# A three-stage kernel: the fold of the transform's input moves from the vector engines into the first products

## The chip, the cores and the metric

The kernel runs as one program on one core of a Trainium2 chip. The metric is the device time of one execution in microseconds (us); the figure quoted is the median of several executions.

## The reference

The reference takes `x` (8 batches, 3072 positions, 256 channels). It computes the real part of the two-dimensional discrete Fourier transform of each batch. The result, 24576 tokens of 256 numbers, goes through a dense layer pair (`softplus(x @ w_in) @ w_out`, 2048 hidden units), and then through a mixture of 8 experts: each token goes to the expert with the largest cosine similarity, and comes out as `relu(x @ w1[e]) @ w2[e]` times that expert's softmax weight.

```python
X = np.fft.fft(x, axis=1); X = np.fft.fft(X, axis=2); a = X.real
h = a @ w_in
a = (np.maximum(h, 0) + np.log1p(np.exp(-np.abs(h)))) @ w_out
e = argmax(normalised(a) @ normalised(emb).T / tau)
out = gate * (np.maximum(a @ w1[e], 0) @ w2[e])
```

## The kernel before, in words

Numbers that have to keep float32's precision are held as two float16 tiles, a high part `h` and a low part `l`, and a product of two such numbers is three TensorE products. To split a float32 tile is therefore two passes: one that scales and rounds to the high part, one that takes the difference.

**Steps.** After a start-up part, phase 1 is a loop of 256 steps, one for each unit (batch, token tile, quarter of the hidden units). Each step issues, in one order written out by hand (`ORDER`, line 56), pieces of several software-pipelined jobs: `pu` and `pv` (28 products of the dense layer's first half), `eu` (ScalarE, L806), `ev` (VectorE, L813 and L814), the softplus on ScalarE (`ab`, `ex`, `ln`: L822, L827, L831) with its last sum on VectorE (`g`, L836), the split of its result into `gh` (GpSimd, L847) and `gl` (VectorE, L860), and `G0` to `G2` (36 products of the second half). The first six steps have orders of their own (`BORD`). SBUF holds all tiles; each engine takes its instructions in this order.

**The transform** of batch b+1 runs in between, as the generator `fft_gen`, one piece at `f1` of each step and now and then one at `f2`. `fft_a` makes 16 pieces for each batch: for each of 8 input tiles `xt` (96 partitions, 4 rows of 256) it multiplies column halves c = 0 and 1 by the table `fa_s` into PSUM tile `psa`, and splits that into `U_s` (L677, L678). I call the steps with such products the A stage of a batch; the steps after them (`psb`, `psc`, `psd`, from `fft_bc`) are the B stage. The A stage of batch 0 belongs to the start-up.

**The fold.** The columns of x come in an order in which half c = 0 needs the sum of the two column halves and half c = 1 their difference. In batch 0 the products make it: per c and row six products, three with each half of the columns, the second half of c = 1 against `fan`, which is `-fa_s`. In batches 1 to 7 the tile is folded first, and per c and row there are three products. The path of one input tile through the steps is: its DMA by `x_get` (SyncE's queue, L585, two buffers `xt`); it is put on the list `late` when the products of the tile two before it are issued; in the next step `sp` folds it (`split_fold`, `x_fold`: sum and difference, L490 to L495), on VectorE for 5 or 6 of the 8 tiles (`FW`, `FW1`) and else on GpSimd with three instructions; at the end of that step `sa` scales it in place and rounds it to `xh`, two ScalarE passes (`split_hi`, L617 and L618); at the head of the step after, `sq` makes `xl` on GpSimd (`split_lo`, L610).

**GpSimd's budget.** At the top of a step `room` is set to `ROOM` (3.6) less 2.6 for a tile that waits for `sq` and 3.4 for one that waits for a fold on GpSimd. A scatter of routed rows (L960) takes 1.4 of it. The preparation of the expert weights (`wprep`, `wp` in the order) runs in chunks that take 2.1 each (L1338 with L1339, or L1343); it also stands still while `busy` is set. `unit_gh` takes 1.2 where that is left (`GPC`): it then makes the last quarter of the low part on GpSimd too (L849, L850, L851; I call it the extra split) and VectorE makes three quarters only.

**Phase 2**, the experts, follows and is not touched, apart from its first pieces, which overlap the last steps.

Of the kernel before, what the change touches and what calls it, by code (L numbers as in the profile page):

```python
# [11 lines left out]
F16 = mybir.dt.float16  # L12
# [3 lines left out]
AF = mybir.ActivationFunctionType  # L16
ALU = mybir.AluOpType
# [18 lines left out]
BOOT = "fbasabpasbpbaaaaabpfbaaaaaambstaaasaabssakaatwaobsfbskskawattaattawaaspfsatat"  # L36
FW, FA = (0, 2, 3, 6, 7), ()
OC = (0, 1, 2, 3, 4, 6, 7)
ROOM = 3.6
FW1, FA1 = (0, 2, 3, 4, 6, 7), ()  # L40
FV = (1, 4, 5, 7)
GP, GPC, GLB = (0, 1, 2, 3), 1.2, 2
# [4 lines left out]
PEF, MK, FB = True, (1, 3, 9, 11, 15), (0, 3, 6, 7)  # L47
# [95 lines left out]
def fft_moe_moe(ctx, tc, x, w_in, w128, w_out, emb, tau, w1, w2, fa, db, mcs, tid, ident, tri, misc, out,  # L143
                nbatch=NB):
    nc = tc.nc
    T, V, A, G, SY = nc.tensor, nc.vector, nc.scalar, nc.gpsimd, nc.sync
# [18 lines left out]
    p1 = ExitStack()  # L165
    pF = ExitStack()
    bigf = pF.enter_context(tc.tile_pool(name="bigf", bufs=1, side="right"))
    U_s = bigf.tile([128, 2, 2, 48, 64], F16, name="U_s")
    mcs_s = bigf.tile([128, 2, 2, 1537], F16, name="mcs_s")
    db_s = bigf.tile([128, 2, 385], F16, name="db_s")  # L170
    fa_s = bigf.tile([96, 2, 96], F16, name="fa_s")
    xp = pF.enter_context(tc.tile_pool(name="xp", bufs=2, side="right"))
    pqp = p1.enter_context(tc.tile_pool(name="pqp", bufs=9))
    big = p1.enter_context(tc.tile_pool(name="big", bufs=1))
# [22 lines left out]
    def fps(name):  # L197

        if boot[2]:
            boot[1] = (boot[1] + 1) % 4  # L200
            if boot[1]:
                return psG.tile([128, 512], F32, tag=f"G{boot[1] - 1}", name=name)
        return psF.tile([128, 512], F32, tag="F", name=name)

    def mm(o, l, r, start, stop):
        T.matmul(o, l, r, start=start, stop=stop)  # L206
# [138 lines left out]
    bootp = boot_ctx.enter_context(tc.tile_pool(name="bootp", bufs=1))  # L345
# [2 lines left out]
    ini = ini_ctx.enter_context(tc.tile_pool(name="ini", bufs=1, side="right"))  # L348
    CK = 512
    wcs = ini.tile([128, NF, 264], F32, name="wcs")  # L350
    fan = bootp.tile([96, 2, 96], F16, name="fan")
    mxw = cst.tile([128, 17], F32, name="mxw")

    def field(i, e11):
# [128 lines left out]
    scal = {}  # L483
# [3 lines left out]
    def x_fold(xt, eng):  # L487

        lo, hi = xt[:, :, 0:128], xt[:, :, 128:256]
        eng.tensor_tensor(lo, lo, hi, op=ALU.add)  # L490
        if eng is V:
            V.scalar_tensor_tensor(hi, hi, -2.0, lo, op0=ALU.mult, op1=ALU.add)
        else:
            G.tensor_scalar(hi, hi, -2.0, 1.0, op0=ALU.mult, op1=ALU.mult)
            G.tensor_tensor(hi, hi, lo, op=ALU.add)  # L495
# [82 lines left out]
    xs, ready = {}, set()  # L578

    def x_get(b, k):  # L580
        if b == 0:
            xs[b, k] = xboot[k]
            return
        xt = xp.tile([96, 4, 256], F32, tag="xt", name="xt", bufs=2)
        SY.dma_start(xt, x[b].rearrange("(p j) d -> p j d", j=32)[:, 4 * k:4 * k + 4, :])  # L585
        xs[b, k] = xt

    def x_split(b, k):
        xt = xs.pop((b, k))
        sx = scal[b]["sx"][0:96]  # L590
        xh = xp.tile([96, 4, 256], F16, tag="xh", name="xh", bufs=3)
        xl = xp.tile([96, 4, 256], F16, tag="xl", name="xl", bufs=3)
        if k not in FB:
            A.activation(xh, xt, AF.Copy, scale=sx)
            V.scalar_tensor_tensor(xl, xt, sx, xh, op0=ALU.mult, op1=ALU.subtract)
        else:
            G.tensor_scalar(xt, xt, sx, 1.0, op0=ALU.mult, op1=ALU.mult)
            G.tensor_scalar(xh, xt, 1.0, 1.0, op0=ALU.mult, op1=ALU.mult)
            G.tensor_tensor(xl, xt, xh, op=ALU.subtract)
        xs[b, k] = (xh, xl)  # L600

    def on_v(b, k):
        return k in (FW1 if b == 1 else FW)

    sp2, sp3 = [], []

    def split_lo():
        for b, k, xt, xh in sp3:
            xl = xp.tile([96, 4, 256], F16, tag="xl", name="xl", bufs=3)
            G.tensor_tensor(xl, xt, xh, op=ALU.subtract)  # L610
            xs[b, k] = (xh, xl)
        sp3.clear()

    def split_hi():
        for b, k, xt in sp2:
            xh = xp.tile([96, 4, 256], F16, tag="xh", name="xh", bufs=3)
            A.activation(xt, xt, AF.Copy, scale=scal[b]["sx"][0:96])  # L617
            A.activation(xh, xt, AF.Copy)  # L618
            sp3.append((b, k, xt, xh))
        sp2.clear()  # L620

    def split_fold():


        for b, k in late:
            xt = xs.pop((b, k))
            x_fold(xt, V if on_v(b, k) else G)
            sp2.append((b, k, xt))
        late.clear()

    def fft_pre(b):

# [11 lines left out]
    def fft_a(b):  # L644

        ph[0] = "a"
        while b not in ready:
            yield
        for k in range(8):
            if k + 2 < 8:  # L650
                x_get(b, k + 2)
            while late and late[0] == (b, k) or sp2 and sp2[0][:2] == (b, k) or sp3 and sp3[0][:2] == (b, k):
                split_lo()
                split_hi()
                split_fold()
            xh, xl = xs.pop((b, k))
            for c in range(2):
                ps = fps("psa")
                for j in range(4):
                    o = ps[:, j * 96:(j + 1) * 96]  # L660
                    cs = slice(c * 128, (c + 1) * 128)
                    if boot[0] and PEF:

                        for hf in range(2):
                            cs = slice(hf * 128, (hf + 1) * 128)
                            fs = fan if c and hf else fa_s
                            mm(o, xh[:, j, cs], fs[:, 0, :], hf == 0, False)
                            mm(o, xh[:, j, cs], fs[:, 1, :], False, False)
                            mm(o, xl[:, j, cs], fs[:, 0, :], False, hf == 1)
                        continue  # L670
                    mm(o, xh[:, j, cs], fa_s[:, 0, :], True, False)
                    mm(o, xh[:, j, cs], fa_s[:, 1, :], False, False)
                    mm(o, xl[:, j, cs], fa_s[:, 0, :], False, True)
                src = ps[:, 0:384].rearrange("p (t q) -> p q t", q=48)
                uh = U_s[:, 0, c, :, 8 * k:8 * k + 8]
                ul = U_s[:, 1, c, :, 8 * k:8 * k + 8]
                A.activation(uh, src, AF.Copy, scale=2.0 ** -16)  # L677
                V.scalar_tensor_tensor(ul, src, 2.0 ** -16, uh, op0=ALU.mult, op1=ALU.subtract)  # L678
                if c == 0 and k + 2 < 8:
# [297 lines left out]
    p2 = {}  # L977
# [379 lines left out]
    def chain(*gens):  # L1357
        for g in gens:
            yield from g

    with tc.manual_schedule():
# [5 lines left out]
        xl = x_load()  # L1367
# [23 lines left out]
        def once(fn, *a):  # L1391
            fn(*a)
            yield
# [9 lines left out]
        def need(t):  # L1403
            while step(t):
# [4 lines left out]
                  t=chain(*(once(win_split, k, h) for k in range(4) for h in range(2))), m=emb_prep(), o=wout_prep())  # L1409
# [37 lines left out]
        sc, scb = Chain(iter(())), [1]  # L1447
        fg = Chain(chain(bg["a"], fft_gen(1)) if nbatch > 1 else bg["a"])
        rq = []
        wp = Chain(iter(()))  # L1450
        for s in range(len(units) + LAG + 1):

            room[0] = ROOM - 2.6 * len(sp3) - 3.4 * sum(not on_v(*t) for t in late)
            nsc = min(len(scq), 2 if cur[0] // 8 >= npair - SNAP or len(scq) > 5 else 1) if room[0] > 0 else 0
            room[0] -= 1.4 * nsc
            busy[0] = bool(sp3) or room[0] < 2.1
            u = units[s] if s < len(units) else None
            if u is not None and u[1] == 0 and u[2] == 0 and 0 < u[0] < nbatch - 1:
                fg.gen = chain(fg.gen, fft_gen(u[0] + 1))
            if s == 4 and nbatch > 1:  # L1460
                sc = Chain(fft_first(1))
# [17 lines left out]
            if ph[0] == "b" and ph[1] + 1 < nbatch and scb[0] < ph[1] + 1:  # L1479
                end_chain(sc)  # L1480
                scb[0] = ph[1] + 1
                sc = Chain(fft_first(ph[1] + 1))
            boot[2] = s < MB
            if s == LAG + 3:
# [5 lines left out]
                wp = Chain(chain(wprep(wpp), snapshot())) if P2ON else Chain(wprep(wpp))  # L1490
# [3 lines left out]
            def x2(tt):  # L1494
                if v is not None and v[2] == 3:
                    x2_out(v[0], v[1], tt)
# [31 lines left out]
            def cv(k):  # L1528
                if s < LAG + 3:
                    wi.step(k)  # L1530
# [9 lines left out]
            def tail():  # L1540
                if "row1" in p2 and (u is None or not S2[0].get("xs")):
# [5 lines left out]
                       ln=lambda: on(unit_ln, 1), g=lambda: on(unit_g, 1), gh=lambda: on(unit_gh, 1),  # L1547
                       lv=lambda: on(unit_gl, 2),
                       G0=lambda: g2(0), G1=lambda: g2(1), G2=lambda: g2(2), x0=lambda: x2(0), x1=lambda: x2(1),
                       x2=lambda: x2(2), r1=route, r2=route, r3=route, sp=split_fold, sa=split_hi, sq=split_lo, wp=wp.step, sc=lambda: scatters(nsc), p1=tail, p2=tail, p3=tail,  # L1550
                       wo=boot_w, cb=lambda: cv(0), ck=lambda: cv(1), cp=lambda: cv(2))
            for o in BORD[s].split() if s < len(BORD) else ORDER:
                ops[o]()
# [51 lines left out]
```

## Time and profile before

| | |
|---|---|
| time, 3 executions | 3482.34 to 3485.62 us, median 3485.12 us |
| the profiled execution's own time | 3496.98 us |
| its span | 3495.2 us |
| TensorE busy | 3078.9 us, 88% of the span |
| VectorE (DVE) busy | 2796.1 us, 80% |
| ScalarE (ACT) busy | 2260.5 us, 65% |
| GpSimd (POOL) busy | 2138.7 us, 61% |
| granted TensorE clock, mean | 0.957 of full speed |

Names of engines in the rows: PE is TensorE (PEld its weight loads), DVE is VectorE, ACT is ScalarE, POOL is GpSimd, SP is SyncE. A line of a timeline gives the start, the duration, the engine, the line of the kernel, the operation, what it writes and reads, and in brackets how long the engine sat idle just before and what ended that. A line of the view of one tile gives the count and the least, the median and the longest duration in ns. All products are recorded under L206, the helper that issues them, so they are told apart by their tiles.

### The profile page before, as it was taken

Reading aid. Unit: us, or ns where it says so; the run is one execution under the profiler, and the core shown is the slowest. Engines: PE = TensorE matmul, PEld = TensorE weight load, DVE = VectorE, ACT = ScalarE, POOL = GpSimd, SP = SyncE. Lnnn points to the kernel's source line nnn. Section 1 sums busy time; section 2 is a strip of 40 time slices with the busy share of each in tenths; the row PEclk is TensorE's granted clock in tenths of the full one; section 3 lists DMA queues with packets and bytes.
Section 4 is the critical chain, followed back from the end, with each engine's and each line's share of the span. In section 5 each row is a group of like instructions: output and inputs, shape, how many; then the busy total and the mean of one; then the engine's idle time right before and its main releaser. Section 6 shows DMA issues by size and latency. Waiting matters only on the chain.

```text
span 3495.2 us, 76414 instructions
## 1 busy us (share of the span) xinstructions
PE 3078.9 (88%) x31264; PEld 2740.8 (78%) x31264; DVE 2796.1 (80%) x4488; ACT 2260.5 (65%) x3400; POOL 2138.7 (61%) x1855
## 2 busy tenths in 40 slices
PE   3788898888987988888988999998889999999997
PEld 3677787876876877777887899877778888888886
DVE  7779898988888989988988988984557777777776
ACT  5777777767877878867877888763344444444443
POOL 5357677776786777777777787662234444444443
PEclk8899998998999999999999999999899999999999
DMA  4111210311211211211111000114643333332221
GB/s 138 48 49 53 71 57 28 101 40 38 73 52 51 80 42 62 80 46 51 50 46 31 19 17 20 65 38 107 175 117 76 75 75 80 75 75 74 73 73 38
DMA packets 197088, 223.74 MB, mean 64 GB/s; under 512 B 119028, under 2 KB 154751, under 8 KB 196480
## 3 DMA queue, kind: packets, MB, share of 16 engines
q1 hardware_dynamic: 177920, 167.32, 18.1%
q0 software_dynamic: 18816, 51.54, 4.2%
q8 instruction: 244, 4.00, 0.5%
q14 instruction: 108, 0.88, 0.1%
HBM read 122.91 MB, written 70.71 MB: 55 GB/s over the span
## 4 chain that ended last, share of the span: by engine, by line
issue 29%; PE 24%; DVE 20%; POOL 12%; ACT 10%; DMA 4%; POOLq 0%; SPq 0%; DVEq 0%; ACTq 0%
PE G L206 12%; DVE e L836 5%; PE pu L206 4%; POOL out_dram L1235 3%; DVE gl L860 3%; PE pv L206 3%; ACT e L831 2%; POOL gh L847 2%; ACT e L827 2%; DVE h L814 2%; DVE h L813 2%; PE psb L206 2%; PE psH L206 1%; ACT e L822 1%; POOL xt L495 1%
## 5 line engine op out<-in xcount | busy, mean ns | idle before, releaser
L847 POOL TENSOR_SCALAR gh<-e,sc 128x1536 f16<-128x1536 f32 (+1 forms) x256 | 620.8, 2425 | 493.5 <-DVE e L836 333.2
L206 PE MATMUL G<-wo_s,gh 128*128 128x264 f16 x6144 | 832.7, 284 | 2.2 <-POOL gh L850 2.0
L206 PEld LDWEIGHTS <-gh 128*128 128x128 f16 x6144 | 602.7, 101 | 100.2 <-POOL gh L850 3.3
L206 PE MATMUL psH<-xT,wb 128*128 128x256 f16 (+1 forms) x4992 | 560.3, 274 | 67.1 <-DMA xT<-xs 66.5
L836 DVE SCALAR_TENSOR_TENSOR e<-h,e 128x1536 f32<-128x1536 f32 x256 | 531.6, 2077 | 75.3 <-ACT e L831 71.8
L206 PEld LDWEIGHTS <-wb 128*128 128x128 f16 x4992 | 480.2, 100 | 137.7 <-DMA xT<-xs 78.3
L206 PEld LDWEIGHTS <-win_s 128*128 128x128 f16 x6144 | 534.0, 100 | 24.6 <-DVE h L814 11.6
L206 PE MATMUL psO<-wb,hh 128*128 128x256 f16 x3200 | 529.8, 273 | 0.6 <-ACT hh L1209 0.6
L206 PE MATMUL G<-wo_s,gl 128*128 128x264 f16 x3072 | 440.3, 281 | 28.6 <-DVE gl L860 28.4
L1147 POOL TENSOR_TENSOR nr<-ssq,half 128x2 f32<-128x2 f32 (+1 forms) x104 | 237.5, 2284 | 355.3 <-ACT jk L1144 355.0
L860 DVE SCALAR_TENSOR_TENSOR gl<-e,sc,gh 128x1536 f16<-128x1536 f32 (+1 forms) x256 | 451.0, 1762 | 3.6 <-POOL gh L847 2.2
L206 PE MATMUL psO<-wb,hl 128*128 128x256 f16 x1600 | 436.2, 273 | 0.6 <-DVE hl L1210 0.5
L1209 ACT ACTIVATE hh<-psH 128x512 f16<-128x512 f32 (+1 forms) x416 | 239.6, 579 | 269.7 <-PE psH L206 263.8
L1210 DVE SCALAR_TENSOR_TENSOR hl<-psH,hh 128x512 f16<-128x512 f32 (+1 forms) x416 | 268.7, 666 | 181.4 <-ACT hh L1209 173.3
L822 ACT ACTIVATE e<-h 128x1536 f32<-128x1536 f32 x256 | 378.0, 1477 | 47.7 <-DVE h L814 46.7
L1235 POOL DMA_INDIRECT out_dram<-ot,r x200 | 202.3, 1011 | 311.2 <-ACT ot L1233 272.3
L831 ACT ACTIVATE e<-e 128x1536 f32<-128x1536 f32 x256 | 379.5, 1482 | 4.0
L827 ACT ACTIVATE e<-e 128x1536 f32<-128x1536 f32 x256 | 378.4, 1478 | 0.0
L206 PE MATMUL pu<-pqh,win_s 128*128 128x192 f16 (+1 forms) x2048 | 371.6, 251 | 3.8 <-ACT h L806 3.8
L206 PEld LDWEIGHTS <-gl 128*128 128x128 f16 x3072 | 303.3, 100 | 89.0 <-DVE gl L860 38.5
L206 PEld LDWEIGHTS <-hh 128*128 128x128 f16 x3200 | 312.6, 98 | 36.8 <-ACT hh L1209 0.7
L813 DVE SCALAR_TENSOR_TENSOR h<-pv,sc,h 128x768 f32<-128x768 f32 (+1 forms) x256 | 258.7, 1011 | 99.2 <-ACT h L806 50.5
(274 smaller groups left out, 5902.8 us busy)
## 6 DMA issues: line engine op xcount, KB each, us to landing
xt<-in_x_dram SPq DMA_DIRECT2D x114, 384.0 KB
r<-bucket SPq DMA_DIRECT2D x96, 268.0 KB
wt<-in_w_dram SPq DMA_DIRECT2D x16, 1024.0 KB
wsc<-wo SPq DMA_DIRECT2D x32, 512.0 KB
W<-wsc SPq DMA_DIRECT2D x32, 512.0 KB
raw<-in_w_in_dram SPq DMA_DIRECT2D x8, 512.0 KB
raw<-in_w_out_dram SPq DMA_DIRECT2D x8, 512.0 KB
wb<-wsc SPq DMA_DIRECT2D x2, 2048.0 KB
```

Source lines behind the costliest of these rows:

```text
L206: T.matmul(o, l, r, start=start, stop=stop)
L813: V.scalar_tensor_tensor(h[:, :, n:384], pv[:, :, s0:n], sc["ninv"], h[:, :, s0:n], op0=ALU.mult, op1=ALU.add)
L822: A.activation(e, h, AF.Abs)
L827: A.activation(e, e, AF.Exp, scale=-1.0)
L831: A.activation(e, e, AF.Ln, bias=1.0)
L836: V.scalar_tensor_tensor(flat(d["e"]), flat(d["h"]), 0.0, flat(d["e"]), op0=ALU.max, op1=ALU.add)
L847: G.tensor_scalar(gh[:, 0:n], e[:, 0:n], sg, 1.0, op0=ALU.mult, op1=ALU.mult)
L860: V.scalar_tensor_tensor(flat(d["gl"]), flat(d["e"]), scal[u[0]]["sg"], flat(d["gh"]), op0=ALU.mult, op1=ALU.subtract)
L1147: G.tensor_tensor(nr[:, 0:nt], ssq[:, 0:nt], half[:, 0:nt], op=ALU.pow)
L1209: A.activation(h2, p_, AF.Relu)
L1210: V.scalar_tensor_tensor(l2, p_, 0.0, h2, op0=ALU.max, op1=ALU.subtract)
L1235: no_dep(G.indirect_dma_start(out=out, out_offset=bass.IndirectOffsetOnAxis(ap=rows.bitcast(I32)[:, t, 264:265], axis=0), in_=ot, in_offse ...
```

## The change

The fold of `xt` is left out in all batches; the products make it as they do in batch 0 (six per c and row in place of three), so `fan` moves to a pool that lives through phase 1. The split becomes one ScalarE pass (`xh`, scaled and rounded, at `sa` of the step in which the tile is put on `late`) and one VectorE pass (`xl`, scaled and subtracted, at `sq` of the next step). `sp` does nothing any more. `room` starts at 4.8 in every step, and `busy` is no longer set within the loop.

```diff
-ROOM = 3.6
+ROOM = 4.8
...
+    fan = bigf.tile([96, 2, 96], F16, name="fan")
...
+    def split_hi():
+        for b, k in late:
+            xt = xs.pop((b, k))
+            xh = xp.tile([96, 4, 256], F16, tag="xh", name="xh", bufs=3)
+            A.activation(xh, xt, AF.Copy, scale=scal[b]["sx"][0:96])
+            sp3.append((b, k, xt, xh))
+        late.clear()
     def split_lo():
         for b, k, xt, xh in sp3:
             xl = xp.tile([96, 4, 256], F16, tag="xl", name="xl", bufs=3)
-            G.tensor_tensor(xl, xt, xh, op=ALU.subtract)
+            V.scalar_tensor_tensor(xl, xt, scal[b]["sx"][0:96], xh, op0=ALU.mult, op1=ALU.subtract)
             xs[b, k] = (xh, xl)
-    def split_hi():
-        for b, k, xt in sp2:
-            xh = xp.tile([96, 4, 256], F16, tag="xh", name="xh", bufs=3)
-            A.activation(xt, xt, AF.Copy, scale=scal[b]["sx"][0:96])
-            A.activation(xh, xt, AF.Copy)
-            sp3.append((b, k, xt, xh))
-    def split_fold():
-        for b, k in late:
-            xt = xs.pop((b, k))
-            x_fold(xt, V if on_v(b, k) else G)
-            sp2.append((b, k, xt))
...
-                    if boot[0] and PEF:
+                    if PEF:
                         for hf in range(2):
...
-            room[0] = ROOM - 2.6 * len(sp3) - 3.4 * sum(not on_v(*t) for t in late)
+            room[0] = ROOM
             nsc = min(len(scq), 2 if cur[0] // 8 >= npair - SNAP or len(scq) > 5 else 1) if room[0] > 0 else 0
             room[0] -= 1.4 * nsc
-            busy[0] = bool(sp3) or room[0] < 2.1
...
-  sp=split_fold, sa=split_hi, sq=split_lo
+  sp=lambda: None, sa=split_hi, sq=split_lo
```

## Rows read from the trace of the kernel before

**Rows 1.** The seven A stages, 100 steps: length, then busy time by engine

```profile
sum 895.90, PE 760.84 PEld 672.49 DVE 800.21 ACT 681.07 POOL 656.18; mean PE 108.69 PEld 96.07 DVE 114.32 ACT 97.30 POOL 93.74
```

**Rows 2.** The same, six stretches of three steps, a batch's first two tiles

```profile
sum 209.60, PE 150.87 PEld 132.66 DVE 170.44 ACT 135.72 POOL 167.56; mean PE 25.14 PEld 22.11 DVE 28.41 ACT 22.62 POOL 27.93
```

**Rows 3.** The same, the last B stage (16 steps), then 20 steps after

```profile
1983.30:2102.40 119.10, 119.10 (x1394) 110.08 (x1393) 102.27 (x118) 99.78 (x117) 95.21 (x97) 1.00 0.05 16
2108.30:2236.20 127.90, 127.90 (x1297) 117.34 (x1296) 113.37 (x112) 108.83 (x96) 96.39 (x90) 1.00 0.06 21
```

**Rows 4.** Waits from 200 to 2110 us: us in total, times, longest

```profile
ACT xt L617 <- POOL xt L495: 105.6, 17, 9.1
```

**Rows 5.** Timeline of ScalarE, one wait for a fold

```profile
534.10 1.15 ACT L617 ACTIVATE xt<-xt,sc 96x1024 f32<-96x1024 f32 x1 [6.72 <-POOL xt L495]
```

**Rows 6.** Timeline of GpSimd, the next `gh`, with VectorE out of the way

```profile
534.05 1.54 POOL L847 TENSOR_SCALAR gh<-e,sc 128x1536 f16<-128x1536 f32 x1
```

**Rows 7.** Timeline of VectorE, two sums of the softplus

```profile
589.56 3.75 DVE L836 SCALAR_TENSOR_TENSOR e<-h,e 128x1536 f32<-128x1536 f32 x1 [0.82 <-ACT e L831]
...
597.40 4.13 DVE L836 SCALAR_TENSOR_TENSOR e<-h,e 128x1536 f32<-128x1536 f32 x1
```

**Rows 8.** Timeline of GpSimd, what ran beside these two

```profile
589.53 2.15 POOL L610 TENSOR_TENSOR xl<-xt,xh 96x1024 f16<-96x1024 f32 x1
...
597.76 2.14 POOL L1343 TENSOR_TENSOR wo<-wt,wo 128x1024 f16<-128x1024 f32 x1
```

**Rows 9.** Timeline of TensorE, one set of 12 products and its follower

```profile
605.57 0.25 PE L206 MATMUL psa<-fa_s,xh 96*128 96x96 f16 x2
...
606.08 0.25 PE L206 MATMUL pu<-pqh,win_s 128*128 128x192 f16 x1
```

**Rows 10.** Tile e: instructions, count, least/median/longest ns

```profile
L836 DVE SCALAR_TENSOR_TENSOR e<-h,e x256: 1736/1759/4910, 122.2 to 2334.1; 128x1536 f32<-128x1536 f32 x128
L847 POOL TENSOR_SCALAR gh<-e,sc x256: 1217/2636/3615, 124.0 to 2338.5; 128x1152 f16<-128x1152 f32 x68, 128x1536 f16<-128x1536 f32 x60
L860 DVE SCALAR_TENSOR_TENSOR gl<-e,sc,gh x256: 1395/1804/4339, 141.4 to 2346.2; 128x1152 f16<-128x1152 f32 x68, 128x1536 f16<-128x1536 f32 x60
L849 POOL TENSOR_SCALAR e<-e,sc x115: 574/580/2301, 125.2 to 2334.0; 128x384 f32<-128x384 f32 x115
L850 POOL TENSOR_SCALAR gh<-e x115: 510/510/1886, 125.9 to 2334.7; 128x384 f16<-128x384 f32 x115
L851 POOL TENSOR_TENSOR gl<-e,gh x115: 908/916/2368, 126.5 to 2336.6; 128x384 f16<-128x384 f32 x115
```

**Rows 11.** Instructions of tile xt, and who waited for it (us, times)

```profile
L617 ACT ACTIVATE xt<-xt,sc x56: 1132/1142/1152, 212.0 to 1951.7; 96x1024 f32<-96x1024 f32 x56
...
L610 POOL TENSOR_TENSOR xl<-xt,xh x56: 2116/2142/3727, 220.9 to 1963.0; 96x1024 f16<-96x1024 f32 x56
L490 DVE TENSOR_TENSOR xt<-xt x36: 676/685/2622, 209.3 to 1948.7; 96x512 f32<-96x512 f32 x36
L492 DVE SCALAR_TENSOR_TENSOR xt<-xt x36: 686/1515/2507, 211.0 to 1949.4; 96x512 f32<-96x512 f32 x36
...
L494 POOL TENSOR_SCALAR xt<-xt x20: 613/2010/2124, 224.3 to 1924.8; 96x512 f32<-96x512 f32 x20
L495 POOL TENSOR_TENSOR xt<-xt x20: 1262/2640/2867, 225.0 to 1925.5; 96x512 f32<-96x512 f32 x20
...
  DVE xt L490: 0.2, 1
```

**Rows 12.** Instructions of tile xh: the low part on VectorE in batch 0

```profile
L595 DVE SCALAR_TENSOR_TENSOR xl<-xb,sc,xh x4: 1272/1754/3664, 31.6 to 54.4; 96x1024 f16<-96x1024 f32 x4
```

**Rows 13.** Instructions of tile pc, GpSimd's part of the B stage

```profile
L733 POOL TENSOR_SCALAR pqh<-pc x51: 505/518/2020, 182.0 to 2098.3; 128x384 f16<-128x384 f32 x44, 128x386 f16<-128x386 f32 x7
L734 POOL TENSOR_TENSOR pql<-pc,pqh x51: 913/922/2501, 182.6 to 2098.9; 128x384 f16<-128x384 f32 x44, 128x386 f16<-128x386 f32 x7
```

**Rows 14.** Instructions of tile wo: one of the two chunks of weight preparation

```profile
L1343 POOL TENSOR_TENSOR wo<-wt,wo x32: 2132/2142/3715, 310.8 to 1706.9; 128x1024 f16<-128x1024 f32 x32
```

More of the change, by code (lines that the diff above doesn't have):

```diff
@@ L350, in fft_moe_moe @@
     wcs = ini.tile([128, NF, 264], F32, name="wcs")
-    fan = bootp.tile([96, 2, 96], F16, name="fan")
     mxw = cst.tile([128, 17], F32, name="mxw")
@@ L600, in x_split @@
         xs[b, k] = (xh, xl)
-    def on_v(b, k):
-        return k in (FW1 if b == 1 else FW)
-    sp2, sp3 = [], []
+    sp3 = []
+    def split_hi():
[5 more added lines that the diff above has]
+        late.clear()
     def split_lo():
@@ L609, in split_lo @@
             xl = xp.tile([96, 4, 256], F16, tag="xl", name="xl", bufs=3)
-            G.tensor_tensor(xl, xt, xh, op=ALU.subtract)
+            V.scalar_tensor_tensor(xl, xt, scal[b]["sx"][0:96], xh, op0=ALU.mult, op1=ALU.subtract)
             xs[b, k] = (xh, xl)
         sp3.clear()
-    def split_hi():
-        for b, k, xt in sp2:
-            xh = xp.tile([96, 4, 256], F16, tag="xh", name="xh", bufs=3)
-            A.activation(xt, xt, AF.Copy, scale=scal[b]["sx"][0:96])
-            A.activation(xh, xt, AF.Copy)
-            sp3.append((b, k, xt, xh))
-        sp2.clear()
-    def split_fold():
-        for b, k in late:
-            xt = xs.pop((b, k))
-            x_fold(xt, V if on_v(b, k) else G)
-            sp2.append((b, k, xt))
-        late.clear()
     def fft_pre(b):
@@ L651, in fft_a @@
                 x_get(b, k + 2)
-            while late and late[0] == (b, k) or sp2 and sp2[0][:2] == (b, k) or sp3 and sp3[0][:2] == (b, k):
+            while late and late[0] == (b, k) or sp3 and sp3[0][:2] == (b, k):
                 split_lo()
                 split_hi()
-                split_fold()
             xh, xl = xs.pop((b, k))
@@ L1549, in fft_moe_moe @@
                        G0=lambda: g2(0), G1=lambda: g2(1), G2=lambda: g2(2), x0=lambda: x2(0), x1=lambda: x2(1),
-                       x2=lambda: x2(2), r1=route, r2=route, r3=route, sp=split_fold, sa=split_hi, sq=split_lo, wp=wp.step, sc=lambda: scatters(nsc), p1=tail, p2=tail, p3=tail,
+                       x2=lambda: x2(2), r1=route, r2=route, r3=route, sp=lambda: None, sa=split_hi, sq=split_lo, wp=wp.step, sc=lambda: scatters(nsc), p1=tail, p2=tail, p3=tail,
                        wo=boot_w, cb=lambda: cv(0), ck=lambda: cv(1), cp=lambda: cv(2))
```

## The prediction, made before the change was run

> **What bounds the kernel now.** I read the page first: no engine fills the span, TensorE at 88% and VectorE at 80% come nearest, so the bound has to be read by stage. The change touches steps 10 to 206 of phase 1 directly and, through GpSimd's budget, all later ones. So I cut the trace at the starts of L806, one for each step, and read busy time by stretch. The reader is to see two things. Where the transform is over, a step takes 127.9 / 20 = 6.40 us and TensorE is busy throughout; in the last B stage 119.1 / 16 = 7.44 us, again all TensorE [rows 3]. In the seven A stages a step takes 895.9 / 100 = 8.96 us with TensorE busy for only 761 of 896 [rows 1], and around a batch's first two tiles, whose split falls into the B stage, 209.6 / 18 = 11.6 us [rows 2]. The products those steps hold would take 6.40 + 0.51 in an A step (12 products of `psa` start at 605.57, the next product at 606.08 [rows 9]). So about 2 us of an A step, and 4 of the others, are waits.
>
> The view of waits names the largest that belongs to the transform: ScalarE stood 105.6 us, 17 times, before its scaling until the last fold instruction on GpSimd was done [rows 4]; one such wait of 6.72 us ends at 534.10 [rows 5]. ScalarE works in order, so the next step's softplus stands behind it. The timelines of VectorE and GpSimd side by side show the second: the softplus sum takes 1.76 us at the median, but 3.75 us beside a subtraction `xl` of 2.15 us on GpSimd, and 4.13 us beside a weight chunk of 2.14 us that begins 0.36 us after it [rows 7, 8, 10]. The excess is the length of GpSimd's instruction. The two engines take turns where VectorE reads two SBUF tiles: a shared path. VectorE instructions that read PSUM are not stretched.
>
> **The change, part by part.**
>
> *Folds.* 36 on VectorE (0.69 + 0.69 us undisturbed) and 20 on GpSimd (1.26 + 0.61 + 1.26 = 3.13) go [rows 11], and with the latter the 105.6 us of ScalarE's wait.
>
> *Split.* 56 subtractions of 2.14 us on GpSimd and 56 scalings of 1.14 us on ScalarE go [rows 11]; the ScalarE pass that stays scales as well, and I take it at the scaling's 1.14 us. VectorE gets 56 passes of this form: 1.27 us at the least, 3.66 at the longest, in batch 0 [rows 12]. I take 1.27, since what stretched the longest was GpSimd, which now has less to do; the other end is in the range. The pass stands at the head of VectorE's step, before `U_s`, `ev` and both softplus passes. It waits for `sa`, the end of ScalarE's step before; VectorE has `g` (1.76) and `gl` (1.4) to do between ScalarE's `ln` and that point, and `sa` takes 1.14, so I cost the wait at nothing. If ScalarE falls behind, `ev` and TensorE's `pv` buffer wait with it.
>
> *Queues.* `sa` now comes in the step that puts the tile on the list, one step earlier, and `sq` too; the DMA of `xt` into one of two buffers waits for `xl`, also one step earlier, so its lead stays the same. Folds hardly ever waited for that DMA (0.2 us, once [rows 11]): nothing. SyncE's queue holds weight loads behind these DMAs; they go no later.
>
> *Products.* 7 batches x 16 sets x 12 = 1344 more. Twelve took 0.51 us [rows 9], 43 ns each: 57 us if TensorE is the bound. An A step then cannot be under 6.40 + 0.51 + 0.51 = 7.42 us. [...]
>
> *Budget.* With 4.8 and no deductions, almost every step makes the extra split, today 115 of 256 [rows 10]. On the shared path one costs GpSimd 1.22 + 0.57 + 0.51 + 0.91 = 3.21 in place of 1.54 [rows 6, 10], and saves VectorE 1.80 - 1.40 = 0.40: net 1.27 us. The 64 chunks of weight preparation (L1338 with L1339, and 32 of L1343, about 2.14 us each [rows 14]) are no longer held back by `busy`; I estimate that they end some 40 steps earlier.
>
> **The sum.** Shared path in an A step with extra split and no chunk: 1.76 + 1.40 + 3.21 + 1.27 / 2 = 7.0 us. In the last B stage it is 1.76 + 1.40 + 3.21 + (0.52 + 0.92) / 2 = 7.1 [rows 10, 13], and that stage runs at 7.44 us a step, 1.05 of it [rows 3]. So I take 7.45 for the 45 A steps of batches 5 to 7, which have few or no chunks left: 335 us. In the 55 A steps before, I estimate a chunk in every second step: (7.0 + 1.07) x 1.05 = 8.5, together 467. That is 802 against 896: 94 less. In the six stretches of rows 2 the path holds 7.1 + 2 x 1.27 / 3 = 7.9, times 1.05 is 8.3 (6 steps), and 9.45 with half a chunk (12 steps): 163 against 210, 46 less. Against this, I estimate 20 chunk steps of the B stages that newly make the extra split: 20 x 1.27 x 1.05 = 27 us more. The last batch scatters two tiles a step (`nsc`), 6 for each of its 4 pairs of token tiles, so in 12 steps, which make the extra split now: 5.1 + 1.27 on the path, times 1.05, is 0.3 over 6.40, 4 us more. Sum: -94 - 46 + 27 + 4 = -109. The profiled execution took 3496.98, 11.9 over the median of 3485.12, so 3388 on its scale is **3376 us** on the median's. Its own range, for chunks in a quarter or in three quarters of the steps and for 0 to 40 new extra splits, is 3325 to 3430.
>
> **Rivals.**
>
> *TensorE alone bounds.* The chunks slip into gaps, as the 64 do in part today. Then 100 A steps take 7.42 (154 less) and the 18 others 7.44 (76 less): 3485 - 230 = 3255 us. For it: TensorE fills 16 B steps entirely while GpSimd makes the extra split in most [rows 3]. Against it: those steps have no chunks.
>
> *The chunk takes the subtraction's place.* A softplus sum that stood behind `xl` on GpSimd stands behind a chunk of the same 2.14 us [rows 7, 8, 14], since nothing keeps the two jobs apart any more. Then only ScalarE's waits are won, 105.6 less the 57 of the products: 3485 - 49 = 3436.
>
> *Slower: the shared path is the bound and the budget spends more than the folds free.* Freed on the path: 56 x 2.14 + 20 x 3.13 + 36 x 1.38 - 56 x 1.27 = 161 us. All 141 further extra splits cost 141 x 1.27 = 179, so 18 us more, times 1.05: 3485 + 19 = 3504. It decides from 127 new splits on, and only where the path, not the wait for the fold, sets the steps. For it: batches 1 to 4, where chunks add to the path. Against it: ScalarE's 105.6 us is waiting, not path time, and goes anyhow. [...]
>
> *No effect.* The tile's path is off the critical one and the short steps behind each long one make the waits good: 3485. Against it, the stage means above contain the short steps already.
>
> **How the numbers follow.** Chances: the forecast 0.57, TensorE alone 0.10, the chunk in place of the subtraction 0.15, no effect 0.04, slower 0.14. A measurement of this kernel can tell about 0.2%, 7 us, from no change. Faster by more than that: 0.57 + 0.10 + 0.15 = 0.82, less 0.01 for a chunk case that eats the 49 us: 0.81. Same: 0.05. Slower: 0.14. The range of 8 in 10 takes in the forecast's own, the chunk case and its price up to 3470, and below it the part of TensorE's case in which some chunk steps stay long, down to 3275; the bound of 3.66 us for `xl`, 56 x 2.4 = 134 more, lies just outside, at 3510, with the slower case.
>
> **What would show it.** In the changed profile: no L617, L490 to L495 or L610 in batches 1 to 7; ScalarE's wait for a fold gone; 12 further products of `psa` in about 0.51 us; L595's twin 56 times at about 1.3 us; L851 well over 115 times; the last A stage at 7.45 us a step with TensorE busy throughout, and those of batches 1 to 4 near 8.5; the last weight chunk some 40 steps earlier. I am wrong if A steps stay near 9 us: with VectorE's sum at 3.7 us beside L1343 or L851 it is the shared path, with TensorE busy throughout it is a higher price of the products, with `ev` late behind the new pass it is its place in the queue.

## The result and the profile after

The changed kernel took 3448.21 us (median of 4 executions, 3443.95 to 3453.37) against 3485.37 for the kernel before in the same session: ratio 0.9889, 95% interval 0.9862 to 0.9916, so 37 us less. The forecast was 109 less, 3376. The direction holds, the size does not: 3448 lies outside the range that the forecast gave for its own mechanism, 3325 to 3430, and inside the wide one only because that took in a rival's price up to 3470. One execution of the kernel before (8188.66 us) and one with the weights' transfers on GpSimd's queue (6948.94 us) were in a slower state and are left out of every median and ratio here. In all rows below, lines are those of the changed kernel: `eu` L794, `g` L824, `gh` L835, extra split L837 to L839, `gl` L848, weight chunks L1326 with L1327 and L1331, all products L207.

The page of the kernel after, its first part (busy time, share of the span, instructions):

```profile
PE 3107.7 (90%) x32608; PEld 2783.0 (81%) x32608; DVE 2694.7 (78%) x4472; ACT 2206.2 (64%) x3344; POOL 2220.2 (64%) x2159
```

By this page little has happened: TensorE 29 us more (1344 more products, at a mean granted clock of 0.967 of full speed against 0.957), VectorE 101 less, GpSimd 82 more. The stages tell more. The windows of the kernel after: the sum over the 55 A steps of batches 1 to 4 (length, then busy time by engine), the A stages of batches 5, 6 and 7 (15 steps each), and the sum over the six stretches that answer to [rows 2]:

```profile
sum 513.50, PE 451.14 PEld 403.62 DVE 430.26 ACT 354.17 POOL 400.83; mean PE 112.78 PEld 100.90 DVE 107.56 ACT 88.54 POOL 100.21
...
1321.50:1443.70 122.20, 116.17 (x1373) 105.43 (x1371) 105.39 (x122) 95.19 (x97) 100.81 (x93) 0.99 0.15 46
1573.70:1685.80 112.10, 111.83 (x1347) 103.75 (x1346) 99.41 (x108) 94.24 (x93) 84.87 (x85) 1.00 0.13 37
1820.40:1932.60 112.20, 111.93 (x1349) 103.85 (x1348) 98.73 (x107) 94.09 (x92) 86.71 (x85) 1.00 0.10 30
...
sum 165.90, PE 143.31 PEld 126.53 DVE 149.10 ACT 122.66 POOL 128.46; mean PE 23.89 PEld 21.09 DVE 24.85 ACT 20.44 POOL 21.41
```

[rows 1] cut in the same way, batches 1 to 4 and batches 5 to 7 of the kernel before:

```profile
sum 514.60, PE 429.34 PEld 378.62 DVE 446.46 ACT 380.24 POOL 365.42; mean PE 107.34 PEld 94.66 DVE 111.61 ACT 95.06 POOL 91.36
...
sum 381.30, PE 331.50 PEld 293.86 DVE 353.75 ACT 300.83 POOL 290.76; mean PE 110.50 PEld 97.95 DVE 117.92 ACT 100.28 POOL 96.92
```

The reader is to see where the gain is missing. Batches 6 and 7 run at 112.1 / 15 = 7.47 us a step with TensorE busy throughout. The A stages of batches 5 to 7 are 346.5, 35 less; the six stretches 44 less. But the A steps of batches 1 to 4 take 513.5 where they took 514.6: nothing came of the removed folds there. And GpSimd, which lost 20 folds and 56 subtractions, is busier in them, 400.83 against 365.42, that is 7.29 us in each of 55 steps, nearly the whole 7.42 that the forecast's estimate gives TensorE for one.

The view of waits, 200 to 2110 us, of the kernel after (total, times, longest):

```profile
ACT xh L609 <- DMA xt<-in_x_dram: 54.6, 6, 15.8
DVE wpm L1301 <- DMA wt<-in_w_dram: 44.0, 13, 4.7
PE pv L207 <- DVE wpm L1304: 43.8, 15, 4.6
PE G L207 <- POOL gh L838: 27.6, 27, 1.3
...
ACT xj L526 <- DMA xt<-in_x_dram: 23.2, 4, 10.9
DVE gl L848 <- POOL gh L835: 22.3, 17, 3.3
```

ScalarE's wait for a fold, 105.6 us [rows 4], is gone. New ones stand in its place. Their worst place is around 780 us, where one step, from 762.9 to 785.3, took 22.4 us. First GpSimd's timeline there (start, us, line, operation, in brackets the idle time before), the `gh` and the two L1331 chunks alone:

```profile
741.89 1.22 POOL L835 TENSOR_SCALAR gh<-e,sc 128x1152 f16<-128x1152 f32 x1
...
749.56 2.14 POOL L1331 TENSOR_TENSOR wo<-wt,wo 128x1024 f16<-128x1024 f32 x1
751.68 1.22 POOL L835 TENSOR_SCALAR gh<-e,sc 128x1152 f16<-128x1152 f32 x1
...
761.10 2.83 POOL L835 TENSOR_SCALAR gh<-e,sc 128x1152 f16<-128x1152 f32 x1
...
771.25 2.13 POOL L1331 TENSOR_TENSOR wo<-wt,wo 128x1024 f16<-128x1024 f32 x1
773.37 1.23 POOL L835 TENSOR_SCALAR gh<-e,sc 128x1152 f16<-128x1152 f32 x1
...
790.93 2.43 POOL L835 TENSOR_SCALAR gh<-e,sc 128x1152 f16<-128x1152 f32 x1 [8.50 <-DVE e L824]
```

Then SyncE's timeline, VectorE's and ScalarE's at the same place; ScalarE's first row is `eu` of the step that issues this last chunk:

```profile
751.72 22.09 SPq L1332 DMA_DIRECT2D wsc<-wo  x2
773.85 0.47 SPq L1296 DMA_DIRECT2D wt<-in_w_dram  x1
774.43 10.84 SPq L585 DMA_DIRECT2D xt<-in_x_dram  x3
```

```profile
780.78 1.22 DVE L1301 TENSOR_REDUCE wpm<-wt 128x1 f32<-128x1024 f32 x1 [4.42 <-DMA wt<-in_w_dram]
```

```profile
755.22 0.90 ACT L794 ACTIVATE h<-pu,sc 128x768 f32<-128x768 f32 x1 [0.83 <-PE pu L207]
...
782.47 1.15 ACT L609 ACTIVATE xh<-xt,sc 96x1024 f16<-96x1024 f32 x1 [15.79 <-DMA xt<-in_x_dram]
```

From one `gh` to the next GpSimd needed 9.79, 9.42 and 12.27 us (differences of the starts), with a `gh`, an extra split, a scatter and a chunk in each, and in the first and third also a piece of the transform (L721, L722); the steps meanwhile took 7.4 to 7.7. At the shortest durations that this timeline has for the same instructions the three would come to some 23.6 us, 7.9 each (an estimate); the other 7.9 of the 31.48 are instructions that ran longer, like the `gh` of 2.83. It fell behind until the last chunk ended at 773.38, 18.2 us after the start of its step at 755.22. SyncE's first row joins two stores: one went out at 751.72, the next only when the last chunk was done, and for some 21 us between them SyncE issued nothing; the load of the next weights and the loads of `xt` come behind. VectorE's two maxima come one and two steps behind the load in the program (`wp` stands twice in a step) and waited, ScalarE waited for `xt`, and then GpSimd, with nothing to do, idled 8.50.

Two readings fit this. **Theory 1**: the place of `xt` in SyncE's queue is the cost. **Theory 2**: GpSimd has too much in the chunk steps, and the budget of 4.8 put it there. A **theory 3**, that the added products cost more than priced, and a **theory 4**, that the weights' load needs a longer lead, were tried beside them.

### The profile page after: what moved, and what is told of

It reads as the page before. It is cut to its first block, busy times and chain, and to the rows that moved or that the text cites. A ratio compares the mean times of both kernels' runs of the same rounds, so it can differ in the third digit from the quotient of the medians.

```text
span 3450.2 us, 79326 instructions
## 1 busy us (share of the span) xinstructions
PE 3107.7 (90%) x32608; PEld 2783.0 (81%) x32608; DVE 2694.7 (78%) x4472; ACT 2206.2 (64%) x3344; POOL 2220.2 (64%) x2159
## 4 chain that ended last, share of the span: by engine, by line
PE 35%; issue 20%; POOL 19%; DVE 11%; DMA 7%; ACT 7%; SPq 0%; POOLq 0%; DVEq 0%; ACTq 0%
PE G L207 15%; PE psH L207 5%; PE pu L207 4%; PE pv L207 3%; PE psO L207 3%; POOL bucket L948 3%; DVE e L824 3%; POOL out_dram L1223 3%; POOL gh L835 3%; PE psa L207 2%; POOL gl L839 2%; DMA xT<-xs 2%; DMA xt<-in_x_dram 2%; POOL gh L838 2%; POOL wo L1331 2%
## 5 line engine op out<-in xcount | busy, mean ns | idle before, releaser
L207 PE MATMUL G<-wo_s,gh 128*128 128x264 f16 x6144 | 828.3, 282 | 38.3 <-POOL gh L838 32.3
L835 POOL TENSOR_SCALAR gh<-e,sc 128x1152 f16<-128x1152 f32 (+1 forms) x256 | 497.9, 1945 | 398.3 <-DVE e L824 346.6
L207 PEld LDWEIGHTS <-gh 128*128 128x128 f16 x6144 | 594.7, 100 | 141.1 <-POOL gh L838 41.1
L207 PE MATMUL psH<-xT,wb 128*128 128x256 f16 (+1 forms) x4992 | 555.8, 273 | 61.7 <-DMA xT<-xs 61.5
L207 PEld LDWEIGHTS <-wb 128*128 128x128 f16 x4992 | 477.6, 99 | 129.8 <-DMA xT<-xs 72.6
L824 DVE SCALAR_TENSOR_TENSOR e<-h,e 128x1536 f32<-128x1536 f32 x256 | 499.8, 1952 | 100.9 <-ACT e L819 98.1
L207 PEld LDWEIGHTS <-win_s 128*128 128x128 f16 x6144 | 529.7, 99 | 24.6 <-issue 14.5
L207 PE MATMUL psO<-wb,hh 128*128 128x256 f16 x3200 | 530.4, 273 | 0.9 <-ACT hh L1197 0.9
L1135 POOL TENSOR_TENSOR nr<-ssq,half 128x2 f32<-128x2 f32 (+1 forms) x104 | 238.2, 2290 | 346.6 <-ACT jk L1132 346.5
L207 PE MATMUL G<-wo_s,gl 128*128 128x264 f16 x3072 | 434.4, 278 | 8.3 <-DVE gl L848 6.8
L207 PE MATMUL psO<-wb,hl 128*128 128x256 f16 x1600 | 436.3, 273 | 0.9 <-DVE hl L1198 0.5
L848 DVE SCALAR_TENSOR_TENSOR gl<-e,sc,gh 128x1152 f16<-128x1152 f32 (+1 forms) x256 | 395.3, 1544 | 24.3 <-POOL gh L835 24.3
L207 PE MATMUL pu<-pqh,win_s 128*128 128x192 f16 (+1 forms) x2048 | 368.2, 250 | 4.6 <-ACT h L794 4.6
L207 PEld LDWEIGHTS <-gl 128*128 128x128 f16 x3072 | 302.3, 99 | 59.9 <-DVE gl L848 9.8
L801 DVE SCALAR_TENSOR_TENSOR h<-pv,sc,h 128x768 f32<-128x768 f32 (+1 forms) x256 | 259.0, 1012 | 113.8 <-PE pv L207 71.9
L207 PEld LDWEIGHTS <-hh 128*128 128x128 f16 x3200 | 312.7, 98 | 37.4 <-ACT hh L1197 1.4
```

The lines of the kernel that those rows point to most:

```text
L801: V.scalar_tensor_tensor(h[:, :, n:384], pv[:, :, s0:n], sc["ninv"], h[:, :, s0:n], op0=ALU.mult, op1=ALU.add)
L824: V.scalar_tensor_tensor(flat(d["e"]), flat(d["h"]), 0.0, flat(d["e"]), op0=ALU.max, op1=ALU.add)
L835: G.tensor_scalar(gh[:, 0:n], e[:, 0:n], sg, 1.0, op0=ALU.mult, op1=ALU.mult)
L848: V.scalar_tensor_tensor(flat(d["gl"]), flat(d["e"]), scal[u[0]]["sg"], flat(d["gh"]), op0=ALU.mult, op1=ALU.subtract)
L1135: G.tensor_tensor(nr[:, 0:nt], ssq[:, 0:nt], half[:, 0:nt], op=ALU.pow)
```

## The experiments

The runs fall into three sessions, in which the kernel before took 3491.59, 3488.13 and 3488.41 us. Ratios are to that kernel in the same session.

**Loads of `xt` on ScalarE's queue**

```diff
-                        SY.dma_start(pair[i], ...)
+                        A.dma_start(pair[i], ...)
-        SY.dma_start(xt, x[b]...)
+        A.dma_start(xt, x[b]...)
```

> Edit: the loads of the input blocks xt are issued from ScalarE's queue instead of SyncE's; the weights' loads and stores stay on SyncE. Theory 1 (the loads of xt stand in SyncE's queue behind the store and the load of the weights, which wait for GpSimd's last chunk): ScalarE's waits for xt (54.6 us in front of the split, 23.2 us in front of the squares) fall under 25 us together and the kernel comes to 3370 to 3410 us. Theory 2 (the steps are long because GpSimd has extra splits and chunks in the same steps): 3440 to 3455, the long steps stay. Theory 3 (the added products are the whole price): 3440 to 3455.

Measured: 3443.52 us, ratio 0.9861 (0.9845 to 0.9878), not told apart from 0.9889. Its view of waits, 200 to 2110 us:

```profile
PE pv L207 <- DVE wpm L1304: 50.8, 15, 4.7
DVE wpm L1301 <- DMA wt<-in_w_dram: 47.2, 13, 6.9
...
ACT xj L526 <- DMA xt<-in_x_dram: 1.0, 1, 1.0
```

ScalarE's waits for `xt` fell from 77.8 to 1.0 us, as theory 1 had it, and the time stayed. Another wait ends in the same steps: VectorE's for the weights and TensorE's behind it. Theory 1 named a real wait that decides nothing.

**The weights' transfers on GpSimd's queue**

```diff
-                SY.dma_start(wt.rearrange(...), w2[e]...)
+                G.dma_start(wt.rearrange(...), w2[e]...)
...
-                SY.dma_start(dst[:, :, cs], wo)
+                G.dma_start(dst[:, :, cs], wo)
```

> Edit: the loads and stores of the weights are issued from GpSimd's queue, so that SyncE carries the loads of xt alone. Theory 1: as with the loads of xt on ScalarE's queue, 3370 to 3410 us, less what GpSimd pays to issue 48 transfers. Theory 2: GpSimd is the engine that is late, so more work on it makes 3450 to 3480. Theory 3: 3440 to 3455.

Measured: 3468.34 us, 0.9934 (0.9915 to 0.9954), slower than the changed kernel by 20 us in the medians, 16 by the ratios. Two waits of it:

```profile
DVE gl L848 <- POOL gh L835: 56.1, 36, 5.2
...
PE G L207 <- POOL gh L835: 26.0, 22, 3.4
```

They were 22.3 and 5.5 us. GpSimd pays some 0.8 us for each of 48 issues (medians there: 799 ns for the 32 of L1332, 764 and 943 for the 8 each of L1296 and L1294), and with more work it is later: theory 2.

**The former budget alone**

```diff
-            room[0] = ROOM
+            room[0] = 3.6 - 2.6 * len(sp3)
...
+            busy[0] = bool(sp3) or room[0] < 2.1
```

> Edit: the budget of the shared path as before (3.6, less 2.6 for a waiting split, chunks barred while a split waits or under 2.1), with the new split and the products kept. Theory 1: the weights' transfers come in other steps, but still ahead of xt in the queue; ScalarE's waits for xt stay over 40 us and VectorE gets the extra splits' work back: 3430 to 3470 us. Theory 2: the steps over 14 us go away, 3340 to 3400. Theory 3: 3440 to 3455.

Measured: 3349.70 us, 0.9607 (0.9579 to 0.9635). The new budget alone costs 98 us. The sum over the 55 A steps of batches 1 to 4:

```profile
sum 452.80, PE 430.90 PEld 392.98 DVE 421.05 ACT 353.44 POOL 300.06; mean PE 107.72 PEld 98.25 DVE 105.26 ACT 88.36 POOL 75.02
```

and its waits:

```profile
PE pv L207 <- DVE wpm L1304: 13.0, 12, 3.3
ACT xj L526 <- DMA xt<-in_x_dram: 11.6, 6, 3.7
...
DVE wpm L1301 <- DMA wt<-in_w_dram: 0.8, 1, 0.8
ACT xh L609 <- DMA xt<-in_x_dram: 0.3, 1, 0.3
```

GpSimd has 300.06 / 55 = 5.46 us a step now, the step is 8.23 in place of 9.34, and all four waits shrink though no transfer was moved to another queue. Theory 2 is borne out, theory 1's "ScalarE's waits stay over 40 us" is wrong.

**The added products left out** (three of six per row and c; the transform's input is then its first half alone)

```diff
-                        for hf in range(2):
+                        for hf in range(1):
...
-                            mm(o, xl[:, j, cs], fs[:, 0, :], False, hf == 1)
+                            mm(o, xl[:, j, cs], fs[:, 0, :], False, True)
```

> Edit: the three added products per set for the second half of the columns are left out, so the transform's input is its first half alone. Priced at 0.51 us per set, 112 sets, 57 us in all. Theory 3 (the products are what the forecast missed): 72 us or more comes off, 3376 us or under. Theories 1 and 2: what is TensorE's in batches 5 to 7 comes off whole (48 sets, 24 us), in the batches with weights to prepare a part, so 3390 to 3425 us, and the long steps there stay.

Measured: 3428.29 us, 0.9818 (0.9801 to 0.9836): 20 us less (25 by the ratios), under what any theory said. Of it 14 lie in the A stages of batches 5 to 7 (332.5 against 346.5). Its batch 6, to be read against 112.10 above:

```profile
1560.40:1667.90 107.50, 105.28 (x1155) 96.55 (x1153) 99.27 (x107) 93.60 (x93) 85.76 (x85) 0.98 0.13 39
```

That is 4.6 us less, where 15 sets at 0.51 make 7.65. In batch 7 most steps do fall from 7.39 to 6.88, but one of them took 9.96 us in place of 8.02, and the granted TensorE clock over the 15 steps was 0.98 in place of 1.00: a part of what the products leave free went into a wait and a lower clock. Theory 3 falls: the products are not what the forecast missed.

**Only the constant: 3.6**

```diff
-ROOM = 4.8
+ROOM = 3.6
```

> Edit: the constant of the budget 4.8 becomes 3.6, nothing else: a step with a scatter and a chunk has no extra split any more; four chunks still stand in consecutive steps. Theory 2 (in those four steps GpSimd has 9 to 10 us of work, 729.85 to 771.25 without a gap, and falls behind; the step is 7.4): without the extra split they hold about 6 us, GpSimd keeps up, 3340 to 3380 us. Theory 4 (what counts is the lead of the weights' load alone: it starts with the last chunk, two steps ahead of the maxima, and four chunks in consecutive steps leave it no more): 3400 to 3450.

Measured: 3358.74 us, 0.9632 (0.9616 to 0.9648). This is the cleanest pair: the last chunk falls in the same step as with 4.8 (step 132), and apart from two of the first chunks, which come one step later, the kernel differs by 98 extra splits alone (157 against 255). The constant keeps them out of the 60 steps that have a chunk with a scatter and the 38 with two scatters. The sum over its 55 A steps of batches 1 to 4:

```profile
sum 477.10, PE 440.40 PEld 397.66 DVE 445.27 ACT 354.19 POOL 344.69; mean PE 110.10 PEld 99.42 DVE 111.32 ACT 88.55 POOL 86.17
```

They are 36 us shorter than as changed, with 15 us more of VectorE's work. GpSimd's timeline and ScalarE's `eu` at the same chunk of the same step as above:

```profile
715.28 3.04 POOL L835 TENSOR_SCALAR gh<-e,sc 128x1536 f16<-128x1536 f32 x1
...
723.26 3.07 POOL L835 TENSOR_SCALAR gh<-e,sc 128x1536 f16<-128x1536 f32 x1
...
730.50 2.14 POOL L1331 TENSOR_TENSOR wo<-wt,wo 128x1024 f16<-128x1024 f32 x1
732.61 3.09 POOL L835 TENSOR_SCALAR gh<-e,sc 128x1536 f16<-128x1536 f32 x1
```

```profile
723.22 0.90 ACT L794 ACTIVATE h<-pu,sc 128x768 f32<-128x768 f32 x1 [0.83 <-PE pu L207]
```

The last chunk ends at 732.64, 9.4 us after the start of its step in place of 18.2. VectorE has no wait for `wt` between 200 and 2110 us any more, with the lead in the program unchanged: theory 4 alone does not hold. TensorE's wait for `wpm` is still 29.3 us, of 43.8.

**A longer lead for the weights' load**

```diff
             yield
             yield
+            yield
+            yield
             m = sm.tile([128, 2], F32, tag="wpm", name="wpm")
```

> Edit: two more idle steps between the issue of the weights' load and the maxima that read it. Theory 4: VectorE's wait for wt, 44.0 us, falls under 10 and TensorE's wait for wpm behind it too, 3360 to 3400 us. Theory 2: GpSimd is behind all the same in the four steps; what TensorE waits for becomes gh and gl of GpSimd, less often since the rhythm is 10 steps: 3410 to 3440.

Measured: 3412.48 us, 0.9778 (0.9762 to 0.9794), 36 us less than the changed kernel. With `wp` twice in a step the two pieces are one step more of lead; the four chunks still come every 8 steps, not every 10, the last in step 133. Its waits:

```profile
ACT xh L609 <- DMA xt<-in_x_dram: 42.6, 7, 8.8
PE G L207 <- POOL gh L838: 36.4, 30, 2.3
...
PE pv L207 <- DVE wpm L1306: 12.2, 15, 1.9
```

The wait for `wt` is gone, and about a third of the loss with it. GpSimd is late all the same, and TensorE's wait for its `gh` rises from 27.6 to 36.4. The lead is a way in which the lateness is paid, not its cause.

**Chunks in every second step, the budget of 4.8 kept**

```diff
-                while busy[0] or not pool_room(2.1):
+                while cur[0] % 2 or not pool_room(2.1):
...
-                while busy[0] or not pool_room(2.1):
+                while cur[0] % 2 or not pool_room(2.1):
```

> Edit: chunks only in every second step, the budget of 4.8 kept, so every step still makes the extra split. Theory 2: two steps of 7.4 us hold two gh, two extra splits, one or two scatters and one chunk, about 14 to 16 us: GpSimd hardly falls behind, 3345 to 3390 us. Theory 4: the last chunk is on time and the load too, about the same. If both are wrong and the extra splits themselves (250 of them) cost the time: 3430 to 3460.

Measured: 3395.46 us, 0.9734 (0.9714 to 0.9754), 5 us over the upper end of theory 2's range. 240 extra splits, only 15 fewer than as changed, and 53 us less: about half of the loss hangs on the four chunks in a row. The edit also draws the chunks out, to step 190, so batches 5 to 7 hold some of them too. The other 46 us down to the former budget's run lie between 240 and 131 extra splits and the other differences of these two; they were not taken apart.

**The new budget on the kernel before**

```diff
-            room[0] = ROOM - 2.6 * len(sp3) - 3.4 * sum(not on_v(*t) for t in late)
+            room[0] = 4.8
...
-            busy[0] = bool(sp3) or room[0] < 2.1
```

> Edit, on the kernel before: its budget becomes the constant 4.8 and the bar on chunks goes, while folds and subtractions stay on GpSimd. Theory 2: GpSimd falls behind here too, and more, with folds, subtractions and extra splits: 3530 to 3620 us. If the budget were no cause, 3485 plus or minus 20.

Measured: 3577.89 us, 1.0262 (1.0244 to 1.0279), 90 us slower than before. The sum over its A steps of batches 1 to 4, and two of its waits:

```profile
sum 568.70, PE 446.69 PEld 391.38 DVE 452.51 ACT 381.51 POOL 458.76; mean PE 111.67 PEld 97.85 DVE 113.13 ACT 95.38 POOL 114.69
```

```profile
ACT xt L617 <- POOL xt L495: 122.4, 18, 10.3
...
DVE wpm L1313 <- DMA wt<-in_w_dram: 30.7, 9, 5.2
```

The budget costs about the same with folds (90) as without (98). So the change is two changes: the split without folds gains 3.9%, 137 us (0.9607), and the budget takes 98 of it back.

**On top of the former budget** four edits were run to see what is left: the longer lead, the longer lead with `xt` on ScalarE's queue, no added products, no extra split (`GP = ()`).

> Edit: the kernel with the former budget and bar (3349.7 us), and two more idle steps between the issue of the weights' load and the maxima. Theory 4: TensorE's wait for wpm, 13.0 us, goes, and the steps with maxima are shorter: 3325 to 3340. Theory 2 (with GpSimd in time the load is in time as well; VectorE waits for wt 0.8 us in two batches): 3340 to 3360.

> Edit: as the run with the former budget and the longer lead, and the loads of xt on ScalarE's queue. Theory 1: ScalarE's 11.6 us of waits for xt go: 10 us under the run with the longer lead. Theory 2: the queue costs nothing that decides once GpSimd is in time, within 5 us of it.

> Edit: the kernel with the former budget, without the three added products per set (the transform's input is its first half alone). If TensorE sets the pace of the steps once GpSimd is in time, the products' price shows whole, 57 us: 3285 to 3300. If they lie in TensorE's gaps, as with the budget of 4.8 (20 us): 3325 to 3340.

> Edit: the kernel with the former budget, without any extra split, so VectorE makes all of gl (1.93 us whole against 1.49 us for three quarters, 0.43 us by 130 steps, 56 us of VectorE). If VectorE's work lies in its gaps: 3340 to 3360. If it sets the pace where the extra split is made now: 3380 to 3405.

Measured: 3345.80 (0.9592, 0.9558 to 0.9626), 3345.61 (0.9595, 0.9560 to 0.9629), 3345.63 (0.9597, 0.9562 to 0.9633) and 3361.07 us (0.9639, 0.9604 to 0.9674). None is told apart from 3349.70; the 130 extra splits save 11 us by the medians, if anything. The first is where theory 2 had it, and the second is within 5 us of it, again theory 2; both beat both kernels, as the former budget alone does. The fourth lies 1 us over the range for VectorE's gaps. The third was a miss: neither expectation had 3346. In batch 7, where TensorE fills most steps, the price is nearly whole, 7.0 us of 7.65; in batch 6, which holds chunks here, only 1.1 is saved (117.8 to 116.7). Batch 7 of that run:

```profile
1728.70:1834.30 105.60, 103.76 (x1156) 95.67 (x1155) 100.76 (x106) 93.67 (x92) 76.05 (x64) 1.00 0.11 32
```

against 112.6 for the same 15 steps with the former budget and the products; single steps go from 7.39 to 6.88 us, by the 0.51 of a set. In batches 1 to 4 only 7 us are saved in the A steps (445.5 against 452.8), and the steps between give it back. What sets those steps was not settled.

Over six of the runs with the new split and all products, the 55 A steps of batches 1 to 4 stand so (sums of the windows by 55; the edit in the first column):

| | GpSimd busy, us a step | length, us a step | whole, us |
|---|---|---|---|
| former budget, no extra split | 5.03 | 8.26 | 3361 |
| former budget | 5.46 | 8.23 | 3350 |
| constant 3.6 | 6.27 | 8.67 | 3359 |
| 4.8, chunks spread | 6.74 | 8.54 | 3395 |
| 4.8, longer lead | 7.46 | 9.12 | 3412 |
| 4.8, as changed | 7.29 | 9.34 | 3448 |

At 5.03 and 5.46 us of GpSimd in a step the length is the same; at 6.3 to 6.7 it is 0.3 to 0.4 us longer, near 7.4 about 1 us, and there GpSimd is the engine that others wait for. The table does not order the runs by itself: a longer lead is shorter with more of GpSimd, and with the chunks spread the cost lies partly in later batches.

## Why the prediction was wrong

*Products.* The price of a set held: 0.51 us where TensorE fills the step. That all 57 us would be paid did not: leaving them out saved 20 us, and 4, not told apart from none, with the former budget. The forecast has no term for TensorE's clock, and with the lower clock the price differs: from 796.12 of the trace after, at a granted clock of 0.50, twelve such products took 0.97 us, where the steps of batch 7 show 0.51 at a granted clock of 1.00 (7.39 less 6.88, with the former budget).

*Folds and split.* ScalarE's 105.6 us are gone, `xl` takes 1.28 us at the median (1.27 forecast), and no wait of it for `sa` came near deciding (8.9 us). The six stretches came to 165.9 against 163 forecast. Batches 6 and 7 came to 7.47 against 7.45. Both hits are in part luck. The factor 1.05 on the shared path was taken from a B stage in which TensorE is busy for all of the 119.10 us [rows 3], and batches 6 and 7 are TensorE's again, so 7.45 does not speak for the path. The stretches came to between 160.1 and 165.9 in all runs with the new split and all products, whatever the budget.

*Budget.* 255 extra splits, and the last chunk 41 steps earlier (step 132 in place of 173), about the 40 that were estimated.

*The step that failed* is in the sum: "In the 55 A steps before, I estimate a chunk in every second step: (7.0 + 1.07) x 1.05 = 8.5, together 467." They took 513.5, 9.34 each. The A stages as a whole gave 860.0 (513.5 + 346.5) against 802, a miss of 58; the six stretches 3; the rest, forecast at +31, came to +35 by the profiles (their spans, 3495.2 and 3450.2, differ by 45.0; the A stages account for 35.9 and the stretches for 43.7; the profiled execution of before stood 11.9 over its median). So the miss is the A stages, 47 us of it in this one term.

"A chunk in every second step" was right: those 55 steps hold 28 chunks. And the sum's own price for a step with a chunk, (7.0 + 2.14) x 1.05 = 9.6, is near the 9.79 and 9.42 that GpSimd needed. What failed is the average, in which each step pays for itself: it charged extra splits and chunks at their undisturbed length on the shared path, half a chunk to each step. The new budget lets four chunks run in consecutive steps with an extra split and a scatter in each, GpSimd falls behind over the four, and the loads and products behind it pay afterwards. Cut at the starts of `eu`, the 27 steps with a chunk took 7.71 us on average, the 28 without one 10.9, and the seven that follow four chunks 14.0 (9.1 with the constant 3.6). The sum never formed what GpSimd itself has to do, scatters and pieces of the transform included: 6.64 us a step before (365.42 / 55), 7.29 after, against a step of 7.42. None of the prediction's signs for A steps near 9 us named GpSimd.

*Queues.* "SyncE's queue holds weight loads behind these DMAs; they go no later" missed the other direction: the loads of `xt` stand behind the store and load of the weights, which wait for GpSimd's last chunk. The wait was real, 54.6 and 23.2 us, but taking it away gained nothing that was measured.

*The rivals.* The slower one, "the budget spends more than the folds free", named the budget, which is the cause, at 98 us where its sum put 179 x 1.05 = 188; the folds freed 137, not 161 x 1.05 = 169. Its way there, the shared path with VectorE, is borne out only in part: in the second pair of [rows 7, 8] the chunk began 0.36 us after VectorE's sum and kept its 2.14 us, and it was the sum that took 4.13, but at 761 of the trace after it is GpSimd's `gh`, the later of the two by 0.05 us, that is longer. Which of the two is held up was not settled. "TensorE alone bounds" is batches 6 and 7. The chunk did not merely take the subtraction's place: that was put at 3436, near the measured 3448, but by VectorE's softplus sum, which the runs do not show as the loss: all 256 sums took 531.6 us before, 499.8 after, and 494.1 with the former budget, 98 us faster. "No effect" is what the A steps of batches 1 to 4 look like, 514.6 and 513.5, but as a gain and a loss that cancel.

## What to carry to other kernels

Where work is moved to or let loose on an engine, add up that engine's own instructions for the steps in question, stretched as the trace shows them, and set the sum against the step: an engine busy for 64% of the span had 7.29 us of work, in one stage, for a step that took 7.47 where TensorE filled it. Look at what arrives in a row, not at the mean: here the last of four chunks in consecutive steps ended 18.2 us after the start of its step, 9.4 with the constant 3.6, and a store, the load of the next weights and the loads of `xt` came behind it. And a long wait in the profile is worth its time only if nothing else ends in the same step: taking ScalarE's 77.8 us away brought no gain that could be told (0.9861 against 0.9889).

## What was not expected of the hardware

The shared path held up GpSimd as well as VectorE. VectorE's softplus sum at the same time as the 2.83 us `gh` above:

```profile
761.05 1.75 DVE L824 SCALAR_TENSOR_TENSOR e<-h,e 128x1536 f32<-128x1536 f32 x1
```

GpSimd's `gh` began 0.05 us after it and took 2.83 us, against 1.22 for the same shape at 751.68: it ended 1.13 us after VectorE's instruction, within 0.09 us of that 1.22. The rows read before the change showed only VectorE's stretch. The trace after agrees with the prediction on which instructions of VectorE are stretched: L824, which reads two SBUF tiles, took 1736 to 4715 ns (256 times), L801 and L802, which read `pv` in PSUM, 996 to 1025 ns (512 times), and L1301, which reads one SBUF tile, 1205 to 1221 ns (32 times).

One store stood some 21 us in SyncE's queue for GpSimd's last chunk, and the loads of `xt` behind it began only at 774.43. Issuing those from ScalarE's queue took ScalarE's waits for them from 77.8 to 1.0 us. Issuing the weights' transfers from GpSimd cost that engine 0.80 us for a store.

After one wait TensorE also ran at a lower clock. It stood still for 4.00 us until 786.01, behind the late loads above. Its products of `pu` and `pv`, 83 ns apart at 787.20, were then 160 ns apart from 787.38 to 790.6, where the granted clock is 0.50. Over the step of 22.4 us and the two behind it the granted clock is 0.92, 0.74 and 0.85. In the 55 A steps of batches 1 to 4 the same products kept TensorE busy for 451.14 us in the changed kernel, at granted clocks of 0.95 to 0.97 by batch, and for 430.90 with the former budget, at 0.97 to 1.00. So 20 of the 61 us that the budget costs in these steps are TensorE's own longer busy time; no run takes the clock apart from the waits, and that the wait brought the lower clock was not shown.
